# Splitting the output projection's weights during the V projection, and taking the last four heads' inverse sums on their output tiles

## The chip, the cores and the metric

The kernel runs on one core of one Trainium2 chip. The metric is the device time of one execution in microseconds. The kernel before takes 1146.8 us (median of three runs, 1144.13 to 1148.85).

## The reference, cut to what matters

One transformer block on x of shape [1, 2048, 640]: sliding-window attention with 32 heads of 20 columns and a window of 256, then a gated MLP that mixes tokens.

```python
def _A_ref(x, wqkv, wo):
    B, S, D = x.shape
    H = 32; Dh = D // H; W = 256
    qkv = (lambda x, *d: x.transpose(*d))((x @ wqkv).reshape(B, S, 3, H, Dh), 2, 0, 3, 1, 4)
    q, k, v = qkv[0], qkv[1], qkv[2]
    scores = jnp.einsum("bhqd,bhkd->bhqk", q, k) * (Dh ** -0.5)
    idx = jnp.arange(S)
    mask = (idx[:, None] - idx[None, :] >= 0) & (idx[:, None] - idx[None, :] < W)
    scores = jnp.where(mask[None, None], scores, -1e9)
    p = _softmax(scores, axis=-1)
    o = jnp.einsum("bhqk,bhkd->bhqd", p, v)
    return (lambda x, *d: x.transpose(*d))(o, 0, 2, 1, 3).reshape(B, S, D) @ wo
...
x = A_x
h = x + _A_ref(_layernorm(x, axis=-1), A_wqkv, A_wo)
h2 = h + _B_ref(_layernorm(h, axis=-1), B_w_in, B_w_sp, B_b_sp, B_w_out)
```

`_B_ref` projects to 1728 columns with a GELU, normalises one half, mixes it over tokens with a 2048x2048 matrix, multiplies with the other half and projects back. The change is in the first half, up to `o @ wo`.

## The kernel before, in words

All tensors are fp32. A product with full precision is made of two fp32r parts, a high one (a rounded copy) and a low one (the rest), as high x high, high x low and low x high. Making the parts of a tile is called a split: one copy and one subtraction.

The stages follow each other. The V projection goes over 16 tiles of 128 tokens: each tile of x is loaded, normalised on DVE, transposed on PE, split by ACT and DVE into the tiles `xa` and `xb`, and multiplied with the split `wv`. Then come the q and k products, whose three-part results go through DRAM (`qk_d`).

Attention takes eight groups g of four heads, and for each 16 tiles of keys, which makes 128 units u. A step s of its loop does four max items for unit s + 17 (a PE product and a row maximum on DVE, L312), four score items for unit s (a PE product and the exponential on ACT, L369; after the fourth, POOL masks the tile, L371 and L374), and the product with V for unit s - 2. A column of ones beside V makes the softmax sum come out as row 20 of a head's 32 output rows. After every fourth unit the function `put` copies 512 tokens of four heads from PSUM into two output tiles `ot{g}_{c}_{j}` (c the 512 tokens, j the half) and stores them in DRAM (`o_d`). Three slots in SBUF hold the operands of a group. Slot 0 and slot 2 lie at the left, slot 2 in the old `xb`; they are free after groups 6 and 5. In the last 17 steps no max items are left, so DVE has only the copies of output tiles.

There also stand, before the change, the preparations for the output projection, in the generators `inverse_sums` and `proj_early`, which advance once per step. `inverse_sums(c)` starts when group 7 has written its output tiles for c: it loads the sums of all 32 heads from `o_d` (`inv`, 128x128), takes the reciprocal on DVE (L348) and stores it in `r_d`. `proj_early` starts at step 112: it loads the five row tiles of `wo` and splits them on DVE (L182, L183) into the tile `t1`, loads the outputs of the first 512 tokens (`load_o`) and then normalises and splits tiles 0 and 1 on DVE (`norm_o` L148, `split_o` L154 and L157). The raw `wo` rows lie for that time in `m1`, where `load_o` loads too, and in `wraw`, where `w_in` is loaded afterwards.

The output projection goes over 16 tiles i: PE multiplies the split outputs with the split `wo` (`wo_ps`, L91), DVE adds x (`xh`, L1160) and takes the statistics for the next layer norm (L75, L76), POOL makes the scale, DVE applies it (L81), PE transposes (`ht_ps`, L806) and ACT copies. A PSUM tile of `wo_ps` is free for the product two tiles later when `xh` has read it. Between these stand on DVE, ACT and POOL the split of tile i + 2 and so on, and of `w_in` and the first inputs of the next stage (`zl`, `aw`, L675).

The order of the instructions is the written one on PE, DVE and ACT up to attention's end, and on SP (the queue that issues nearly all DMAs) from attention's start to step 112. Everywhere else a scheduler orders them, and it may put later work between earlier rows. Each engine then runs its own list strictly in order.

## Time and profile before

| | us |
|---|---|
| median of the runs | 1146.8 |
| the profiled execution | 1140.25 |
| its span, first to last instruction | 1138.5 |
| PE busy | 1094.5 |
| DVE busy | 746.0 |
| ACT busy | 534.6 |
| POOL busy | 405.2 |
| attention's last product with V before the output projection starts | 460.10 |
| first and last start of `wo_ps` | 463.8 and 556.4 |

Times within the execution count from its first instruction. Rows of a timeline give the start, the duration, the engine, the line, the operation, what it writes and reads by the program's names (with the numbers at their ends left out, so `t` is `t1` and `m` is `m1`), and in brackets how long the engine was idle before and what ended that. Rows of waits give the total, how often, and the longest.

### The profile page before, as it was taken

Reading aid. Unit: us, or ns where it says so; the run is one execution under the profiler, and the core shown is the slowest. Engines: PE = TensorE matmul, PEld = TensorE weight load, DVE = VectorE, ACT = ScalarE, POOL = GpSimd, SP = SyncE. Lnnn points to the kernel's source line nnn. Section 1 sums busy time; section 2 is a strip of 40 time slices with the busy share of each in tenths; the row PEclk is TensorE's granted clock in tenths of the full one; section 3 lists DMA queues with packets and bytes.
Section 4 is the critical chain, followed back from the end, with each engine's and each line's share of the span. In section 5 each row is a group of like instructions: output and inputs, shape, how many; then the busy total and the mean of one; then the engine's idle time right before and its main releaser. Section 6 shows DMA issues by size and latency. Waiting matters only on the chain. (4 is left out here: it accounts for less than half of the span.)

```text
span 1138.5 us, 27633 instructions
## 1 busy us (share of the span) xinstructions
PE 1094.5 (96%) x10652; PEld 982.7 (86%) x10652; DVE 746.0 (66%) x1963; ACT 534.6 (47%) x1165; POOL 405.2 (36%) x553
## 2 busy tenths in 40 slices
PE   6999999999999999888999998999999899999998
PEld 6998887668888886788999997999999799999998
DVE  5541223889999996599677489455558974556542
ACT  3333433259999999344366454333334421222210
POOL 4114444457777778366230363000126410000000
PEclk9999999999999999899999998999999999999999
DMA  6212565655666635588455411324331572444322
GB/s 197 70 36 86 168 225 165 212 201 187 215 211 204 199 131 193 177 291 269 163 187 182 165 51 37 103 102 136 112 112 53 170 235 91 127 142 145 99 74 78
DMA packets 83845, 170.84 MB, mean 150 GB/s; under 512 B 11009, under 2 KB 47361, under 8 KB 79873
## 3 DMA queue, kind: packets, MB, share of 16 engines
q1 hardware_dynamic: 81408, 163.83, 44.5%
q10 hardware_dynamic: 2304, 5.24, 1.2%
q8 instruction: 83, 1.36, 0.5%
q14 instruction: 50, 0.40, 0.1%
HBM read 112.37 MB, written 56.23 MB: 148 GB/s over the span
## 5 line engine op out<-in xcount | busy, mean ns | idle before, releaser
L369 ACT ACTIVATE pt<-bank 128x384 f32<-128x384 f32 (+2 forms) x512 | 200.7, 498 | 9.3 <-PE bank L366 5.1
L1013 PE MATMUL g<-zl,aw 128*128 128x432 f32 x768 | 174.4, 363 | 7.3 <-ACT zl L681 4.9
L681 ACT ACTIVATE aw<-fx 128x512 fp32r<-128x512 f32 (+2 forms) x160 | 92.7, 595 | 186.6 <-PE g L1013 121.4
L312 DVE CUSTOM_DVE_ANT_0 junk<-bank,strip 128x288 bf16<-128x288 f32 x392 | 157.6, 454 | 3.7 <-PE bank L300 1.4
L1013 PEld LDWEIGHTS g<-zl,aw 128*128 128x128 f32 x768 | 144.9, 190 | 16.1 <-ACT zl L681 5.9
L1013 PE MATMUL g<-ze,aw 128*128 128x432 f32 x576 | 138.2, 368 | 5.1 <-DVE row L675 2.9
L675 DVE TENSOR_TENSOR aw<-fx,aw 128x512 fp32r<-128x512 f32 (+2 forms) x152 | 108.4, 721 | 35.7 <-ACT aw L681 35.4
L394 PE MATMUL pv<-pt,v_sb 128*32 128x192 f32 (+3 forms) x1984 | 127.2, 322 | 2.6 <-POOL pt L371 1.9
L1013 PEld LDWEIGHTS g<-ze,aw 128*128 128x128 f32 x576 | 109.3, 192 | 12.9 <-ACT y_sp L124 1.9
L366 PE MATMUL bank<-slot 123*32 123x288 bf16 (+5 forms) x1536 | 106.6, 280 | 1.9 <-issue 0.7
L371 POOL TENSOR_SCALAR_AFFINE_SELECT pt<-pt 128x512 f32<-128x512 f32 x128 | 84.0, 656 | 45.0 <-ACT pt L369 44.0
L1052 PE MATMUL out_ps<-wout,y_sp 128*128 128x320 f32 (+1 forms) x630 | 96.2, 310 | 0.4 <-ACT y_sp L124 0.4
L1052 PEld LDWEIGHTS out_ps<-wout,y_sp 128*128 128x128 f32 (+1 forms) x630 | 94.1, 188 | 1.3 <-ACT y_sp L124 0.7
L917 PE MATMUL zb<-win,aw 128*128 128x432 f32 x480 | 95.2, 359 | 0.0
L917 PEld LDWEIGHTS zb<-win,aw 128*128 128x128 f32 x480 | 90.1, 188 | 4.4
L300 PE MATMUL bank<-slot 120*32 120x288 bf16 (+2 forms) x1264 | 88.2, 283 | 1.6 <-DVE mcol L312 1.0
L498 DVE TENSOR_TENSOR rest<-qk,sg 128x512 f32<-128x512 f32 x40 | 27.7, 692 | 86.1 <-ACT sg L496 86.0
L374 POOL TENSOR_SCALAR_AFFINE_SELECT pt<-pt 128x512 f32<-128x512 f32 x112 | 72.3, 645 | 0.0
L675 DVE TENSOR_TENSOR row<-g,row 128x432 f32<-128x432 f32 x80 | 48.0, 603 | 36.4 <-PE g L1013 32.0
L501 POOL TENSOR_TENSOR sg<-rest,sg 128x512 bf16<-128x512 f32 x40 | 46.6, 1165 | 69.7 <-ACT sg L500 63.1
L366 PEld LDWEIGHTS <-slot 123*32 123x32 bf16 x1536 | 53.2, 96 | 17.3 <-issue 6.2
L394 PEld LDWEIGHTS pv<-pt,v_sb 128*32 128x32 f32 x1984 | 59.9, 110 | 8.4 <-POOL pt L371 3.8
(189 smaller groups left out, 2172.2 us busy)
## 6 DMA issues: line engine op xcount, KB each, us to landing
fx<-wsp_in SPq DMA_DIRECT2D x32, 512.0 KB
slot<-qk_d SPq DMA_DIRECT2D x72, 200.0 KB
qk_d<-sg SPq DMA_DIRECT2D x32, 384.0 KB
slot<-qk_d SPq DMA_DIRECT2D x72, 160.0 KB
fx<-hn_d SPq DMA_DIRECT2D x32, 320.0 KB
o_d<-ot SPq DMA_DIRECT2D x64, 128.0 KB
z_d<-row SPq DMA_DIRECT2D x16, 432.0 KB
g_d<-row SPq DMA_DIRECT2D x16, 432.0 KB
```

The costliest lines, as they stand in the source:

```text
L300: nc.tensor.matmul(ps[32 * j:32 * j + 32, :n], part(st, half, 120, 0, hh, q0, 32), part(st, half, 120, 1, hh, lo + skip * j, n), start=Tru ...
L312: nc.vector.tensor_tensor_reduce(out=junk[:, :n], in0=ps[:, :n], in1=keep, scale=1.0, scalar=NEG, op0=OP.add, op1=OP.max, accum_out=m_cols ...
L366: nc.tensor.matmul(ps[32 * i:32 * i + 32, b:e], part(st, half, 123, 1, hh, k0, 32), part(st, half, 123, 0, hh, kb * P + b, e - b), start=T ...
L369: nc.scalar.activation(pt[:, hh, :n], ps[:, :n], AF.Exp, scale=SCALE)
L371: nc.gpsimd.affine_select(out=pt[:, :, :P], in_=pt[:, :, :P], pattern=[[0, 4], [1, P]], base=0, channel_multiplier=-1, compare_op=OP.is_ge ...
L374: nc.gpsimd.affine_select(out=pt[:, :, 256:], in_=pt[:, :, 256:], pattern=[[0, 4], [-1, P]], base=-1, channel_multiplier=1, compare_op=OP. ...
L394: nc.tensor.matmul(ps[32 * hh:32 * hh + 32, a - 512 * c:b - 512 * c], v_sb[:, kb, v0:v0 + 32], pt[:, hh, a - kb * P:b - kb * P], start=fir ...
L675: (eng or nc.vector).tensor_tensor(out=out, in0=a, in1=b, op=op)
L681: nc.scalar.activation(out, a, AF.Copy)
L917: nc.tensor.matmul(b[0][:, :HF], a[t][:, x, kk], win2[0][:, y, kk, h * HF:(h + 1) * HF], start=kk + x + y == 0, stop=kk == KD - 1 and x == 1)
L1013: nc.tensor.matmul(ps, w[m][:, x, k], zc[k][m][:, y], start=start and k + x + y == 0, stop=stop and k == 3 and x == 1, skip_group_check=True)
L1052: nc.tensor.matmul(ps[j][:, :HD], src[:w, a, k, :], e1["wout"][:w, b, k, j * HD:(j + 1) * HD], start=(k == 0 and a + b == 0), stop=(k == K ...
```

## The change

Four things are done.

- `wo` is loaded and split during the V projection, in iterations 1 to 7: `load_wo` brings the five row tiles, `split_wo` makes the high part on ACT and the low part on POOL, in buffers that the `wq` tiles use later, and stores both in DRAM (`wo_d`). In attention's steps from 97 on, `load_wo_parts` loads the ten parts, one a step, into `xb`, which has been free since group 5. The loads and splits in `proj_early` go.
- The tile `t1` goes. `wo`'s parts and the split outputs (`osp_parts`) lie in `xb`, which is kept to the end of the projection. `wraw` lies in the pool that `xh2` to `xh4` come from.
- `inverse_sums` serves only the first 28 heads. It starts when group 6, not group 7, has written c, waits five steps before its load and three before the reciprocal.
- For group 7, `put` takes the reciprocal of the whole output tile (`rt`, 128x256, L410 in the new file) and stores its four rows of sums in `r_d`.

```diff
@@ attention's output tiles and inverse sums
         def inverse_sums(c):
-            t = tmp3.tile([P, P], F32, tag="inv", bufs=2, name=f"inv{c}")
+            t = tmp3.tile([P, P], F32, tag="inv", bufs=2, name=f"inv{c}")[:4 * (H - 4)]
 
             def rows(d, step):
-                return bass.AP(tensor=d.tensor, offset=d.offset, ap=[[step, H], [P, 4], [1, P]])
-
+                return bass.AP(tensor=d.tensor, offset=d.offset, ap=[[step, H - 4], [P, 4], [1, P]])
+
+            for _ in range(5):
+                yield
             nc.sync.dma_start(t, rows(o_d[:, DH, c * 512:(c + 1) * 512], 32 * S))
+            for _ in range(3):
+                yield
+            nc.vector.reciprocal(out=t, in_=t)
             yield
-            yield
-            nc.vector.reciprocal(out=t, in_=t)
             nc.sync.dma_start(rows(r_d[:, c * 512:(c + 1) * 512], S), t)
             yield
...
                     nc.sync.dma_start(o_d[4 * g:4 * g + 4, :, e:e + 256].rearrange("h d t -> (h d) t"), ot)
+                    if g == 7:
+                        rt = tmp3.tile([P, 256], F32, tag="rt", bufs=2, name=f"rt{c}_{j}")
+                        nc.vector.reciprocal(out=rt, in_=ot)
+                        nc.sync.dma_start(r_d[4 * g:4 * g + 4, e:e + 256], rt[DH:P:32])
...
-                if g == 7:
+                if g == 6:
                     inverse.append(inverse_sums(c))
@@ wo in the V projection
+            def load_wo(k):
+                raws["o", k] = tmp.tile([P, D], F32, tag="wraw", bufs=4, name=f"woraw{k}")
+                nc.sync.dma_start(raws["o", k], wo[k * P:(k + 1) * P, :])
+
+            def split_wo(k):
+                raw = raws.pop(("o", k))
+                hi, lo = (tmp.tile([P, D], F32R, tag=tag, bufs=4, name=f"{tag}o{k}") for tag in ("wqh", "wql"))
+                nc.scalar.activation(hi, raw, AF.Copy)
+                nc.gpsimd.tensor_tensor(out=lo, in0=raw, in1=hi.bitcast(F32), op=OP.subtract)
+                nc.sync.dma_start(wo_d[0, k], hi.bitcast(F32))
+                nc.sync.dma_start(wo_d[1, k], lo.bitcast(F32))
...
+                if 1 <= i <= KD:
+                    load_wo(i - 1)
...
+                if 3 <= i < KD + 3:
+                    split_wo(i - 3)
@@ the parts in xb
-        mem["t1"] = pl.tile([P, 2 * KF * D], F32R, name="t1")
...
-        mem["wraw"] = pl.tile([P, 2, 2, HF], F32, name="wraw")
...
-    def t1(lo, *shape):
-        return view(mem["t1"], lo, *shape)
+    def wo_part(p, k):
+        return mem["xb"][p][:, k * D:(k + 1) * D]
+
+    def osp_parts(i):
+        if i % 3 == 2:
+            return [x[:, 7 * D:8 * D].rearrange("p (k t) -> p k t", k=KD) for x in mem["xb"]]
+        o = view(mem["xb"][i % 3], KD * D, 2, KD, P)
+        return [o[:, 0], o[:, 1]]
...
+    def load_wo_parts():
+        for k in range(KD):
+            for p in range(2):
+                nc.sync.dma_start(wo_part(p, k).bitcast(F32), wo_d[p, k])
+                yield
...
-        xb = pool(lowx, "xb")
-        xb = [xb.tile([P, CH], F32R, name=f"xb{i}") for i in range(2)]
+        xb = pool(early_stack, "xb")
+        xb = mem["xb"] = [xb.tile([P, CH], F32R, name=f"xb{i}") for i in range(2)]
...
+            if s > 6 * NT:
+                next(wo_loads, None)
...
-    mem["osp2"] = ep.tile([P, 2, KD, P], F32R, name="osp2")
+    mem["wraw"] = ep.tile([P, 2, 2, HF], F32, name="wraw")
@@ proj_early
-        for k in range(KD):
-            raw = raws_c.pop(f"wo{k}")
-            nc.vector.tensor_copy(wo_s[:, 0, k], raw)
-            nc.vector.tensor_tensor(out=wo_s[:, 1, k], in0=raw, in1=wo_s[:, 0, k].bitcast(F32), op=OP.subtract)
-            if k in (1, 3):
-                yield
-        yield
         rs = load_o(0)
-        yield
         yield
         rs()
         yield
-        yield
         load_o(1)()
-        yield
+        for _ in range(6):
+            yield
         for i in range(2):
             norm_o(i, nc.vector)
             split_o(i, nc.vector)
```

Three places show how the rows move. The first is DVE in attention's last steps, from the first output tiles of group 7 on. Before:

```order
L410 COPY ot7_0_1_9100<-pv7_0_8981 128x256
L182 CAST t1_8919<-m1_8920 128x640
L183 TENSOR_TENSOR t1_8919<-m1_8920,t1_8919 128x640
...
L182 CAST t1_8919<-wraw_8926 128x640
L183 TENSOR_TENSOR t1_8919<-wraw_8926,t1_8919 128x640
L348 RECIPROCAL inv0_9107<-inv0_9107 128x128
L410 COPY ot7_1_0_9247<-pv7_1_9061 128x256
L410 COPY ot7_1_1_9250<-pv7_1_9061 128x256
L348 RECIPROCAL inv1_9253<-inv1_9253 128x128
```

Now:

```order
L406 COPY ot7_0_0_9151<-pv7_0_9033 128x256
L410 RECIPROCAL rt0_0_9154<-ot7_0_0_9151 128x256
L406 COPY ot7_0_1_9157<-pv7_0_9033 128x256
L410 RECIPROCAL rt0_1_9160<-ot7_0_1_9157 128x256
L344 RECIPROCAL inv2_8844<-inv2_8844 112x128
L406 COPY ot7_1_0_9297<-pv7_1_9115 128x256
L410 RECIPROCAL rt1_0_9300<-ot7_1_0_9297 128x256
L406 COPY ot7_1_1_9303<-pv7_1_9115 128x256
L410 RECIPROCAL rt1_1_9306<-ot7_1_1_9303 128x256
L344 RECIPROCAL inv3_9021<-inv3_9021 112x128
```

The ten splits of `wo` are gone from here, a reciprocal stands behind each copy of an output tile, and `inv0` and `inv1` have moved ahead (`inv0` among the last row maxima). All reciprocals of the first 28 heads are done before the output tiles for c = 2.

The second place is DVE at the start of the projection; the rows with `m1` are `norm_o`, the row that waits for the most DMAs is the one for tile 2. Before:

```order
L348 RECIPROCAL inv1_9253<-inv1_9253 128x128 [waits DMAHW2_49]
L148 TENSOR_TENSOR m1_8920<-m1_8920 128x5x128 [waits DMAHW4_49,DMAHW3_49,DMAHW7_49,DMAHW1_49,DMAHW0_49]
L154 CAST t1_8919<-m1_8920 128x640 [waits DVE_49]
L157 TENSOR_TENSOR t1_8919<-m1_8920,t1_8919 128x640 [waits DVE_49]
L148 TENSOR_TENSOR m1_8920<-m1_8920 128x5x128
L148 TENSOR_TENSOR m1_8920<-m1_8920 128x5x128 [waits DMAHW4_49,DMAHW5_49,DMAHW3_49,DMAHW7_49,DMAHW1_49,DMAHW0_49]
```

Now:

```order
L410 RECIPROCAL rt2_0_9445<-ot7_2_0_9442 128x256 [waits DMAHW4_49,Activation_49]
L410 RECIPROCAL rt2_1_9451<-ot7_2_1_9448 128x256 [waits DMAHW0_49,DVE_49,Activation_49]
L153 TENSOR_TENSOR m1_8976<-m1_8976 128x5x128 [waits DMAHW5_49,DMAHW2_49,DMAHW1_49]
L153 TENSOR_TENSOR m1_8976<-m1_8976 128x5x128 [waits DMAHW4_49,DMAHW6_49,DMAHW3_49,DMAHW7_49,DMAHW2_49,DMAHW1_49]
L153 TENSOR_TENSOR m1_8976<-m1_8976 128x5x128
L159 CAST xb0_95<-m1_8976 128x640 [waits DVE_49]
```

In place of `inv1`, which waits for a DMA, two reciprocals stand ahead, which wait for ACT; and the normalisations of tiles 2 and 3 have moved ahead of tile 0's cast (tile 1 now comes after it).

The third place is DVE at the first two additions of x. Before:

```order
L348 RECIPROCAL inv2_9398<-inv2_9398 128x128
L1160 TENSOR_TENSOR xh0_8921<-wo_ps0_9473,xh0_8921 128x640
L75 BN_STATS stc0_9608<-xh0_8921 128x6 x2
L76 BN_AGGR mvc0_9609<-stc0_9608 128x2
L81 TENSOR_SCALAR m1_8920<-xh0_8921,mvc0_9609 128x640
L1160 TENSOR_TENSOR xh1_8922<-wo_ps1_9518,xh1_8922 128x640
L75 BN_STATS stc1_9624<-xh1_8922 128x6 x2
L148 TENSOR_TENSOR m1_8920<-m1_8920 128x5x128 x2
L348 RECIPROCAL inv3_9549<-inv3_9549 128x128
```

Now:

```order
L1173 TENSOR_TENSOR xh0_8977<-wo_ps0_9525,xh0_8977 128x640
L76 BN_STATS stc0_9665<-xh0_8977 128x6
L410 RECIPROCAL rt3_0_9570<-ot7_3_0_9567 128x256
...
L153 TENSOR_TENSOR m1_8976<-m1_8976 128x5x128 x2
L410 RECIPROCAL rt3_1_9576<-ot7_3_1_9573 128x256
L77 BN_AGGR mvc0_9666<-stc0_9665 128x2
L1173 TENSOR_TENSOR xh1_8978<-wo_ps1_9579,xh1_8978 128x640
...
L76 BN_STATS stc1_9681<-xh1_8978 128x6 x2
L82 TENSOR_SCALAR m1_8976<-xh0_8977,mvc0_9666 128x640
```

`inv2` and `inv3` are gone, `rt3_0` and `rt3_1` and the normalisations of tiles 4 and 5 now stand ahead of `xh1`, and the use of tile 0's statistics has moved behind `xh1`.

More of the change, by code (lines that the diff above doesn't have):

```diff
@@ L56, in block_kernel @@
     g_d = dram.tile([NT, P, FH], F32, name="g_d")
+    wo_d = dram.tile([2, KD, P, D], F32, name="wo_d")
     ident = const.tile([P, P], F32, name="ident")
@@ L151, in split_o @@
         ot, _ = ots[i]
-        osp = mem["osp2"] if i % 3 == 2 else t1((2 * KD + i % 3 * 2) * D, 2, KD, P)
+        osp = osp_parts(i)
         if eng is nc.vector:
-            eng.tensor_copy(out=osp[:, 0], in_=ot)
+            eng.tensor_copy(out=osp[0], in_=ot)
         else:
-            nc.scalar.activation(osp[:, 0], ot, AF.Copy)
-        eng.tensor_tensor(out=osp[:, 1], in0=ot, in1=osp[:, 0].bitcast(F32), op=OP.subtract)
+            nc.scalar.activation(osp[0], ot, AF.Copy)
+        eng.tensor_tensor(out=osp[1], in0=ot, in1=osp[0].bitcast(F32), op=OP.subtract)
         ots[i] = osp
@@ L161, in proj_o @@
         osp = ots.pop(i)
[L162 to L175 removed]
+        gemm(ps, HD, [lambda k, p=p: osp[p][:, k, :] for p in range(2)],
+             [lambda k, j, p=p: wo_part(p, k)[:, j * HD:(j + 1) * HD] for p in range(2)], KD)
+        return ps
+    def load_wo_parts():
[3 more added lines that the diff above has]
+                yield
+    def proj_early():
         for i in range(2):
             load_x2(i)
[L178 removed]
+        for _ in range(6):
             yield
[L180 to L186 removed]
         rs = load_o(0)
[L188 removed]
         yield
@@ L191, in proj_early @@
         yield
-        yield
         load_o(1)()
-        yield
+        for _ in range(6):
+            yield
         for i in range(2):
@@ L201, in block_kernel @@
     with ExitStack() as ab:
-        lowx, low0, high, x01, b1 = (ab.enter_context(ExitStack()) for _ in range(5))
+        low0, high, x01, b1 = (ab.enter_context(ExitStack()) for _ in range(4))
         tmp2 = pool(high, "tmp2", side="right")
@@ L651, in block_kernel @@
             pass
-        for f in inverse:
-            for _ in f:
-                pass
     ms.close()
```

17 lines of the change are left out of this document (2 added, 15 removed).

## The prediction

> **What bounds the kernel now.** I read the stretches first. The table of windows lists per row the stretch (us), its length, the busy time of PE, PEld, DVE, ACT and POOL with instruction counts, the granted clock, the DMA share and GB/s.
>
> ```profile
> core 0: us, PE busy (x) PEld busy (x) DVE busy (x) ACT busy (x) POOL busy (x), PEclk, DMA share, GB/s
> 20.00:80.00 60.00, 60.00 (x426) 59.93 (x425) 31.35 (x76) 20.25 (x49) 10.26 (x26) 1.00 0.20 56
> 245.00:434.00 189.00, 186.11 (x5282) 153.58 (x5278) 184.44 (x930) 180.21 (x477) 141.93 (x271) 1.00 0.57 183
> 434.00:461.00 27.00, 23.41 (x517) 13.83 (x509) 12.86 (x18) 24.66 (x67) 23.50 (x35) 1.00 0.65 217
> 461.00:472.00 11.00, 8.21 (x50) 7.82 (x51) 8.31 (x10) 1.88 (x4) 2.02 (x2) 0.69 0.54 161
> 472.00:542.00 70.00, 61.60 (x410) 59.37 (x409) 65.69 (x106) 26.54 (x48) 43.08 (x41) 0.98 0.81 266
> 542.00:557.00 15.00, 15.00 (x109) 14.98 (x108) 10.50 (x21) 2.86 (x4) 5.27 (x11) 1.00 0.58 215
> 557.00:1138.50 581.50, 565.04 (x3053) 537.94 (x3051) 360.20 (x603) 210.51 (x400) 96.59 (x84) 0.99 0.37 120
> ```
>
> The V projection (20 to 80) is PE alone. In attention (245 to 434) DVE, with its row maxima, is busy 98%, and PE and ACT nearly as much. In its tail (434 to 461), where no maxima are left, ACT and POOL set the pace. Then comes a hole (461 to 472), and from 472 to 542, the output projection, DVE is at 94% and PE at 88%. The change touches the first five rows; the 581 us behind keep their instructions.
>
> Next, PE's longest wait from 461 to 558 (total, times, longest), and the ends of the projection stage on DVE and on PE:
>
> ```profile
> PE wo_ps L91 <- DVE xh L1160: 6.7, 5, 3.0
> ```
> ```profile
> 540.77 0.81 DVE L1160 TENSOR_TENSOR xh<-wo_ps,xh 128x640 f32<-128x640 f32 x1
> ```
> ```profile
> 541.63 2.46 PE L91 MATMUL wo_ps<-t 128*128 128x320 f32 x15 [1.30 <-DVE xh L1160]
> ```
>
> PE is held by the residual additions `xh`. The one at 540.77 belongs to tile 11; after it PE runs on without a break. So the stage ends when DVE has finished `xh11`, and a microsecond there is a microsecond at the end.
>
> **The change, part by part.** (a) Splitting wo during the V projection adds five ACT copies and five POOL subtractions of 128x640, with ten stores and five loads on SP. The same shapes stand in the trace:
>
> ```profile
> L474 ACT ACTIVATE wqh<-wqraw x10: 729/731/742, 79.3 to 178.0; 128x640 fp32r<-128x640 f32 x10
> L475 POOL TENSOR_TENSOR wql<-wqraw,wqh x10: 1560/1569/1584, 80.1 to 179.8; 128x640 fp32r<-128x640 f32 x10
> ```
>
> That is 5 x 0.73 = 3.7 us on ACT and 5 x 1.57 = 7.8 us on POOL, against 20.3 and 10.3 busy of 60 while PE is full. In ACT's queue each copy stands behind the evacuations that the next product needs. On SP the stores come ahead of later x loads, but those wait for the normalisation three tiles on anyway. Cost 0; with the cover gone it would be 7.8 us. The ten later loads of the parts go out at attention's group 6, spread among o_d stores, where slots are no longer loaded: 0.
>
> (b) The four reciprocals of the first 28 heads come earlier; `inv0` now stands between the last row maxima, where DVE is full:
>
> ```profile
> 420.00:430.00 10.00, 10.00 (x288) 8.21 (x281) 9.84 (x50) 9.71 (x25) 8.16 (x17) 1.00 0.15 46
> ```
> ```profile
> L348 DVE RECIPROCAL inv<-inv x4: 952/953/953, 453.5 to 481.6; 128x128 f32<-128x128 f32 x4
> ```
>
> At most 0.95 us, at least 0 if the banks ahead of it absorb it; I take +0.7.
>
> (c) The ten wo instructions leave DVE at 442.7 to 452.4, and this is where I see the gain. POOL's mask over the same time, DVE's split, and the reciprocal behind it:
>
> ```profile
> 440.73 0.63 POOL L371 TENSOR_SCALAR_AFFINE_SELECT pt<-pt 128x512 f32<-128x512 f32 x1 [0.37 <-ACT pt L369]
> ...
> 442.26 0.63 POOL L371 TENSOR_SCALAR_AFFINE_SELECT pt<-pt 128x512 f32<-128x512 f32 x1 [0.31 <-ACT pt L369]
> ...
> 447.70 1.21 POOL L371 TENSOR_SCALAR_AFFINE_SELECT pt<-pt 128x512 f32<-128x512 f32 x1
> ...
> 453.47 0.63 POOL L371 TENSOR_SCALAR_AFFINE_SELECT pt<-pt 128x512 f32<-128x512 f32 x1
> ...
> 456.21 0.64 POOL L371 TENSOR_SCALAR_AFFINE_SELECT pt<-pt 128x512 f32<-128x512 f32 x1 [0.31 <-ACT pt L369]
> ```
> ```profile
> 447.29 1.13 DVE L183 TENSOR_TENSOR t<-m,t 128x640 fp32r<-128x640 f32 x1
> ...
> 453.50 0.95 DVE L348 RECIPROCAL inv<-inv 128x128 f32<-128x128 f32 x1 [1.07 <-DMA inv<-o_d]
> ```
> ```profile
> ACT pt L369 <- PE bank L366: 0.9, 4, 0.3
> ```
>
> A mask takes 1.21 us instead of 0.63 while DVE casts and subtracts, and 0.63 beside the reciprocal. With the masks late PE is late, and ACT, which sets the tail, idles 0.9 us in four waits. The masks of two tiles start 1.53 us apart at 440.73 and 442.26; the eight tiles from 442.26 to 456.21 took 13.95 instead of 12.24, so the loss is 0.9 to 1.7; I take -1.1. Where the masks waited, only copies from PSUM and reciprocals stand now. [...]
>
> (d) The handover. ACT, DVE and PE there:
>
> ```profile
> 457.40 0.78 ACT L408 ACTIVATE ot<-pv 128x256 f32<-128x256 f32 x2
> ```
> ```profile
> 461.25 0.95 DVE L348 RECIPROCAL inv<-inv 128x128 f32<-128x128 f32 x1 [6.20 <-DMA inv<-o_d]
> 462.12 0.76 DVE L148 TENSOR_TENSOR m<-m 128x640 f32<-128x640 f32 x1
> 462.92 0.82 DVE L154 CAST t<-m 128x640 fp32r<-128x640 f32 x1
> ```
> ```profile
> 460.10 0.53 PE L394 MATMUL pv<-pt,v_sb 128*32 128x192 f32 x8 [0.22 <-POOL pt L371]
> 463.79 7.19 PE L91 MATMUL wo_ps<-t 128*128 128x320 f32 x30 [3.16 <-DVE t L154]
> ```
>
> Before, tile 0's normalisation was stuck on DVE behind `inv1`, which waited 6.20 us for its load. That wait goes, but the order shows what is late next: two reciprocals of 128x256, `rt2_0` and `rt2_1`, now stand there, and they need the output tiles that ACT writes at 457.40; behind them come the normalisations of tiles 0, 2 and 3 before tile 0's cast. No row has a 128x256 reciprocal. Its price lies between 0.95 (no growth with the width) and 1.91 (twice); I take 1.85, almost twice, since 0.95 for 128 columns, against 0.76 for a multiplication of 640 columns at 462.12, says that it is paid by the column. With (b) and (c) the first tile is there at 457.8 - 0.4 = 457.4; 2 x 1.85 + 3 x 0.76 brings the cast to 463.4, and PE starts 0.87 later as before: 464.3 against 463.79, +0.5 (both ends of the reciprocal: -1.3 to +0.6). The normalisation of tile 2 needs loads that stand on SP behind `rt1_1`'s store. The product that ends this tile's sums:
>
> ```profile
> 449.81 0.64 PE L394 MATMUL pv<-pt,v_sb 128*32 128x256 f32 x8 [0.16 <-POOL pt L374]
> ```
>
> From 450.5 two copies of 0.35 and two reciprocals take DVE to 454.9, and the loads have 7 us to land.
>
> The first product takes 7.19 us because of the clock:
>
> ```profile
> 463.00:469.00 6.00, 5.21 (x19) 5.21 (x20) 4.49 (x6) 0.74 (x1) 0.50 (x1) 0.50 0.60 174
> ```
> ```profile
> 471.39 4.67 PE L91 MATMUL wo_ps<-t 128*128 128x320 f32 x30
> ```
>
> Half speed costs it 2.5 us against the second. The hole stays, so I leave that loss: product 0 ends at 464.3 + 7.2 = 471.5. [...]
>
> (e) The projection stage. Before, `inv2` kept DVE, and `xh0` started late, after product 0 had ended at 471.0:
>
> ```profile
> 472.46 0.76 DVE L1160 TENSOR_TENSOR xh<-wo_ps,xh 128x640 f32<-128x640 f32 x1
> ```
>
> Now it starts at 471.5: -0.95. From `xh0` to `xh11` the instructions are the same on both orders, less `inv3` (0.95) and plus `rt3_0` and `rt3_1` (2 x 1.85): +2.75. Against it stands DVE's idle time in that stretch:
>
> ```profile
> DVE m L148 <- DMA m<-o_d: 1.9, 1, 1.9
> DVE m L81 <- POOL mvc L78: 1.7, 2, 1.0
> DVE inv L348 <- DMA inv<-o_d: 1.1, 2, 0.8
> DVE m L148 <- issue: 0.2, 1, 0.2
> ```
>
> 4.9 us, of which 0.8 is `inv2`'s ahead of `xh0`: 4.1. The added reciprocals and an earlier w_in split fill it: `xh1` and two normalisations now stand between a tile's statistics and its use, and the loads of tiles 4 and 5 no longer share SP with `inv2`. I take 3.5 of it back (0 to 4.1): -0.75, bounds +2.75 to -1.35.
>
> Sum: to `xh0` -0.95, which holds (b), (c) and (d); the stage -0.75; -1.7 together. The profiled execution, 1140.25 (span 1138.5), becomes 1138.5. It lies 6.5 below the median shown, 1146.8, which becomes **1145**.
>
> **Rivals.** One, *DVE meets POOL less in the projection stage*, faster. DVE's operations are stretched there too:
>
> ```profile
> L148 DVE TENSOR_TENSOR m<-m 128x640 f32<-128x640 f32 x12 | 10.5, 907 | 2.1 <-DMA m<-o_d 1.9 <-issue 0.2
> L81 DVE TENSOR_SCALAR m<-xh,mvc 128x640 f32<-128x640 f32 x10 | 10.0, 1005 | 1.7 <-POOL mvc L78 1.7
> ```
> ```profile
> L81 DVE TENSOR_SCALAR m<-xh,mvc x10: 553/606/1856, 475.4 to 534.5; 128x640 f32<-128x640 f32 x10
> ```
>
> Against 0.76 (the row at 462.12) and 0.61 (the median) these two groups lose 12 x 0.15 + 10 x 0.4 = 5.8 us. The new order of all rows after attention is another draw. If it saved all of that, -7.5 in total: 1139. Against it: the same POOL work must fit the same stage.
>
> Two, *DVE waits at its head for loads of o*, slower. The normalisations of tiles 4 to 7 now stand one place earlier on DVE, and on SP the loads for 6 and 7 stand behind `rt3_0`'s store, which waits for DVE. If each of the two pairs comes 3 us late, DVE, the bound, loses 6, and `rt3` costs its full 2.75 with nothing recovered: -0.95 + 2.75 + 6 = +7.8, 1154.6. It decides once those loads take over 3.6 us from issue to landing; the row above shows one such wait of 1.9.
>
> Three, *the tail doesn't speed up*, because the reciprocals stretch the masks as the casts did: 1.1 is not gained, the sum is -0.6: 1146.2. The mask of 0.63 at 453.47 beside a reciprocal speaks against it.
>
> **The numbers.** Forecast 0.62, less meeting 0.14, late loads 0.10, no tail gain 0.14. The range takes the bounds (about -5 to +4) and part of the first two rivals, with some spread of the runs, which lie 4.7 apart: 1139 to 1151. What this kernel's measurement can tell from no change is 0.5%, 5.7 us: faster means below 1141.1, slower above 1152.5. Most of rival one is faster, 0.12 in all; most of rival two slower, 0.08; the rest 0.80.
>
> **What would show it.** Masks of 0.63 throughout the tail and no ACT idle there (c); `rt` rows of 1.85 us with the cast right behind `rt2_1` and three normalisations, and PE's start near 464 (d); `xh0` without a wait on DVE and DVE without idle until `xh11`, which ends near 540 (e); PE full to 80 us (a). I am wrong if a reciprocal of 256 columns is far from 1.85, if PE starts before 462, or if DVE waits for o_d loads in the projection.

## The result and the profile after

The changed kernel takes 1150.37 us (median of 14 runs, 1147.76 to 1154.12), the kernel before 1143.95 in its 14 runs: a ratio of 1.0062 with a 95% interval of 1.0046 to 1.0078. It is slower by 0.6%, some 6.4 us. The forecast was 1145, a gain of 1.7; the direction was wrong.

The profiled executions lie 13.9 apart, 1154.12 (span 1152.4) against 1140.25. To see where, cut both at the same five instructions: the start of the last row maximum on DVE, which ends attention's full part, the last product of attention with V, the first product of the output projection, and the first and the last residual addition (`xh0`, `xh15`). The rows of the two DVE ends, the first two of the kernel before, the others of the changed one:

```profile
432.79 0.45 DVE L312 CUSTOM_DVE_ANT_0 junk<-bank,strip 128x288 bf16<-128x288 f32 x1
...
556.77 0.82 DVE L1160 TENSOR_TENSOR xh<-wo_ps,xh 128x640 f32<-128x640 f32 x1 [0.84 <-PE wo_ps L91]
```
```profile
438.45 0.45 DVE L306 CUSTOM_DVE_ANT_0 junk<-bank,strip 128x288 bf16<-128x288 f32 x1
...
480.96 0.82 DVE L1173 TENSOR_TENSOR xh<-wo_ps,xh 128x640 f32<-128x640 f32 x1 [2.90 <-PE wo_ps L92]
...
568.80 0.82 DVE L1173 TENSOR_TENSOR xh<-wo_ps,xh 128x640 f32<-128x640 f32 x1 [0.78 <-PE wo_ps L92]
```

Up to the last row maximum the changed kernel is 5.7 us later, from there to `xh15` 6.4 longer (130.35 against 123.98), and behind `xh15` 1.9 longer. The first and the third piece are mostly the spread of single executions: in the fourteen profiles of this study the last row maximum starts at 432.8 to 436.5 in the four kernels without the new sums and at 434.0 to 441.0 in the ten with them, and what follows `xh15` takes 579.9 to 585.5. The middle piece is the change's, and it alone is as large as the difference of the medians (as near as single executions tell).

The hole in the changed kernel as a window (stretch, length, busy time of PE, PEld, DVE, ACT and POOL with counts, granted clock, DMA share, GB/s), and PE's two ends of it:

```profile
464.60:474.00 9.40, 0.03 (x4) 0.00 (x0) 6.47 (x6) 0.74 (x1) 0.73 (x2) 0.68 0.43 132
```
```profile
464.10 0.53 PE L390 MATMUL pv<-pt,v_sb 128*32 128x192 f32 x8 [0.22 <-POOL pt L367]
474.05 0.90 PE L92 MATMUL wo_ps<-xb 128*128 128x320 f32 x2 [9.42 <-DVE xb L159]
```

PE stands still for 9.4 us between attention and the projection, where it stood 3.16 before. DVE in that hole, first row to last:

```profile
464.72 1.75 DVE L410 RECIPROCAL rt<-ot 128x256 f32<-128x256 f32 x1 [2.34 <-DMA r_d<-rt]
...
471.71 1.56 DVE L153 TENSOR_TENSOR m<-m 128x640 f32<-128x640 f32 x2 [2.11 <-DMA o_d<-ot]
473.19 0.81 DVE L159 CAST xb<-m 128x640 fp32r<-128x640 f32 x1
```

DVE waits three times, twice for the store of an earlier `rt` tile (there are two buffers) and then at the pair of normalisations of tiles 2 and 3, whose data aren't there. The last row names a store of an output tile as what ended that wait; the profile infers this, and in e2_norm_early, e7_rt_copy and e9_rt_own_two the same wait ends with the load of the inverse sums (`m<-r_d`), which is issued here at 468.05. Tile 0's cast, for which PE waits, stands behind that pair.

Piece by piece, from the anchors named: last row maximum to last product with V 25.65 (before 27.3), -1.65; from there to the projection's first product 9.95 (3.69), +6.26; to `xh0` 6.91 (8.67), -1.76; `xh0` to `xh15` 87.84 (84.31), +3.53. Together +6.4.

### The profile page after: what moved, and what is told of

Same layout as the page of the kernel before. It is cut to its first block, busy times and chain, and to the rows that moved or that the text cites. A ratio compares the mean times of both kernels' runs of the same rounds, so it can differ in the third digit from the quotient of the medians.

```text
span 1152.4 us, 27709 instructions
## 1 busy us (share of the span) xinstructions
PE 1096.0 (95%) x10652; PEld 983.6 (85%) x10652; DVE 750.0 (65%) x1961; ACT 538.3 (47%) x1170; POOL 409.3 (36%) x558
## 3 DMA queue, kind: packets, MB, share of 16 engines
q8 instruction: 84, 1.38, 0.5%
## 5 line engine op out<-in xcount | busy, mean ns | idle before, releaser
L362 PE MATMUL bank<-slot 123*32 123x288 bf16 (+6 forms) x1536 | 109.0, 282 | 3.9 <-issue 1.7
L367 POOL TENSOR_SCALAR_AFFINE_SELECT pt<-pt 128x512 f32<-128x512 f32 x128 | 81.5, 637 | 50.4 <-ACT pt L365 49.6
L370 POOL TENSOR_SCALAR_AFFINE_SELECT pt<-pt 128x512 f32<-128x512 f32 x112 | 71.4, 638 | 0.0
```

What stands on the lines that cost most here:

```text
L362: nc.tensor.matmul(ps[32 * i:32 * i + 32, b:e], part(st, half, 123, 1, hh, k0, 32), part(st, half, 123, 0, hh, kb * P + b, e - b), start=T ...
L367: nc.gpsimd.affine_select(out=pt[:, :, :P], in_=pt[:, :, :P], pattern=[[0, 4], [1, P]], base=0, channel_multiplier=-1, compare_op=OP.is_ge ...
L370: nc.gpsimd.affine_select(out=pt[:, :, 256:], in_=pt[:, :, 256:], pattern=[[0, 4], [-1, P]], base=-1, channel_multiplier=1, compare_op=OP. ...
```

## The experiments

Two theories stood after this. *Buffers*: two `rt` buffers are too few, and DVE waits at them. *Order and loads*: tile 0's cast stands behind tiles 2 and 3, whose loads come late for another reason. The table gives the places of each profiled execution, from the start of its last row maximum, and the ratio of the medians; each place comes from one execution.

| kernel | last pv | first wo product | xh0 | xh15 | ratio |
|---|---|---|---|---|---|
| before | 27.3 | 31.0 | 39.7 | 124.0 | 1 |
| changed | 25.65 | 35.6 | 42.5 | 130.35 | 1.0062 |
| e1_rt8 | 25.5 | 31.1 | 39.05 | 124.7 | 1.0057 |
| e2_norm_early | 25.9 | 28.1 | 38.8 | 124.9 | 1.001 |
| e3_wo_only | 32.5 | 33.3 | 39.5 | 123.6 | 1.0011 |
| e4_sums_only | 35.3 | 37.8 | 44.2 | 132.4 | 1.0117 |
| e5_rt_own | 25.5 | 31.5 | 38.2 | 124.7 | 1.0008 |
| e6_norm_rt_own | 25.9 | 26.3 | 34.6 | 118.8 | 0.9973 |
| e7_rt_copy | 25.85 | 32.6 | 39.9 | 125.4 | 1.001 |
| e8_wo_norm_early | 25.6 | 28.45 | 37.1 | 129.9 | 1.005 |
| e9_rt_own_two | 25.5 | 31.4 | 38.15 | 124.2 | 0.9994 |
| e10_norm_rt_load | 25.7 | 26.05 | 35.8 | 118.9 | 0.9958 |
| e11_rt_ho | 25.5 | 35.6 | 42.5 | 130.2 | 1.0058 |
| e12_wo_late | 32.4 | 33.2 | 39.0 | 126.2 | 1.003 |

### e1_rt8: eight buffers for rt

```diff
-  rt = tmp3.tile([P, 256], F32, tag="rt", bufs=2, ...)
+  rt = tmp3.tile([P, 256], F32, tag="rt", bufs=8, ...)
```

> The changed kernel with eight buffers for the inverted output tiles rt instead of two; nothing else. Theory A, the two buffers: in the profile of the change DVE waited 6.7 us in four places for the store of the rt two before. With a buffer for each, those waits go, rt2_0 starts right behind ACT's output copy, PE starts wo_ps0 about 5 us earlier (469 instead of 474) and the time falls from 1150.4 to about 1145.4. Theory B, the order on SP and DVE: between 454.5 and 468.6 SP issues 19 transfers at 0.6 to 0.75 us each, and the loads that tiles 2 and 3 need stand last among them; these two tiles' normalisations stand ahead of tile 0's cast, so DVE then waits there instead, PE starts at 471 to 473, and the time is 1148 to 1149.5. Theory C, attention itself has become slower (its last product ended 4.0 us later in the profile): the handover changes nothing that counts beyond that, and 1150 stays.

Measured: 1148.89 against 1142.54, ratio 1.0057 (1.0039 to 1.0075). The waits at `rt` are gone and the hole is short again, but the time isn't better. The larger pool moved attention's tiles in memory: the first exponentials now wait for a store of a staging tile of q and k (4.09 us), and PE behind them.

```profile
250.70 2.47 ACT L365 ACTIVATE pt<-bank 128x384 f32<-128x384 f32 x6 [4.09 <-DMA qk_d<-sg]
```

So the run doesn't tell the theories apart: what it gained at the handover it lost at attention's start. The time lies in theory B's range, but not for theory B's reason, since DVE waits only 1.38 us at tiles 2 and 3. Nor is the short hole the buffers' doing alone: the larger pool also moved five loads on SP behind the handover (issued at 487.7 to 489.7), the same five that e9_rt_own_two is about.

### e2_norm_early: tiles 0 and 1 normalised ahead

```diff
         rs()
         yield
-        load_o(1)()
-        for _ in range(6):
+        for _ in range(3):
             yield
         for i in range(2):
             norm_o(i, nc.vector)
             split_o(i, nc.vector)
             yield
+        load_o(1)()
```

> The changed kernel with tile 0's and tile 1's normalisation and split asked for earlier (three steps behind the load of the sums, not seven) and the loads for tiles 2 and 3 behind them. On DVE tile 0's normalisation, cast and subtraction now stand ahead of rt2_0 and rt2_1. The rt buffers stay two. Theory B: tile 0 needs only what has long landed, PE starts wo_ps0 at about 464.5, right behind attention's last product; DVE reaches xh0 when rt2, two normalisations and tile 1's split are done, at about 474 to 475 instead of 481; time 1143 to 1145. Theory A: DVE's waits for the rt stores stay and hold rt1 and rt2 as before; PE's early start gains nothing, since xh0 stands behind rt2 on DVE: xh0 at 478 or later, 1147 to 1150. Theory C: 1150, with attention's end where it was.

Measured: 1144.28, ratio 1.001 (0.9993 to 1.0028), no longer slower than before. The waits at `rt` stay (3.29 us at one of them); what changed is that tile 0's cast no longer stands behind tiles 2 and 3. PE's first product:

```profile
465.80 0.61 PE L92 MATMUL wo_ps<-xb 128*128 128x320 f32 x2 [1.68 <-DVE xb L159]
```

The order theory can explain the loss without the buffers.

### e3_wo_only and e4_sums_only: one part alone

The changed kernel with the old `inverse_sums` for all 32 heads and no `rt`:

```diff
-  t = tmp3.tile([P, P], F32, tag="inv", ...)[:4 * (H - 4)]
+  t = tmp3.tile([P, P], F32, tag="inv", ...)
...
-  if g == 7:
-      rt = ...; nc.vector.reciprocal(out=rt, in_=ot); nc.sync.dma_start(r_d[...], rt[DH:P:32])
...
-  if g == 6:
+  if g == 7:
       inverse.append(inverse_sums(c))
```

> The changed kernel with the inverse sums as they were before the change (all 32 heads in one load behind group 7, no rt): the split of wo in the V projection and its loads in parts alone. If the handover is the cost of the change (A and B), this kernel has it not: 1142 to 1144, the tail's 1 us gained or lost in the spread, and a hole of 3 us or less at the handover. If the loads of the wo parts or the stack memory that wo keeps slow attention down (C), attention ends 3 to 4 us later than before here too, and the time is 1147 to 1149.

And the kernel before with the new sums, the same lines the other way round:

```diff
+  t = tmp3.tile([P, P], F32, tag="inv", ...)[:4 * (H - 4)]
...
+  if g == 7:
+      rt = ...; nc.vector.reciprocal(out=rt, in_=ot); nc.sync.dma_start(r_d[...], rt[DH:P:32])
...
-  if g == 7:
+  if g == 6:
       inverse.append(inverse_sums(c))
```

> The kernel before with the new inverse sums alone (28 heads behind group 6, the last four on their output tiles); wo is loaded and split in the tail as before. A and B: rt stands on DVE with its two buffers and the ten wo instructions between them: a hole of 9 us or more at the handover, time 1150 to 1154. C: the hole is there but attention ends where it did before, 1146 to 1148.

Measured: the split alone 1142.78, ratio 1.0011 (0.9996 to 1.0027); the sums alone 1155.42, ratio 1.0117 (1.0096 to 1.0138). The first says that splitting `wo` during the V projection costs nothing, as forecast, and gains nothing by itself: DVE, freed from the splits, only waits for the inverse sums, and ACT's cast of a tile of the projection, in its queue ahead of the last exponentials, holds them, and PE with them (4.79 us at one product of scores).

```profile
462.50 1.56 DVE L153 TENSOR_TENSOR m<-m 128x640 f32<-128x640 f32 x2 [10.19 <-DMA m<-r_d]
```
```profile
463.36 0.74 ACT L161 ACTIVATE xb<-m 128x640 fp32r<-128x640 f32 x1 [4.34 <-DVE m L153]
```

The second missed its expectation of a hole of 9 us: the hole is 1.7, and the loss lies ahead of it, where the last product with V comes 8.0 us later than before. So the new sums need the splits out of the way: with both on DVE, the copy that frees a product's bank is late.

```profile
462.72 0.66 PE L396 MATMUL pv<-pt,v_sb 128*32 128x128 f32 x8 [4.29 <-DVE ot L412]
```

The parts aren't additive (1.0011 and 1.0117 against 1.0062 together).

### e5_rt_own and e6_norm_rt_own: own buffers, without and with the early normalisation

Six `rt` tiles of their own in the pool of the early stage, and two in the old place:

```diff
+  mem["rt"] = [pl.tile([P, 256], F32, name=f"rt{i}") for i in range(6)]
+  mem["rt"] += [tmp3.tile([P, 256], F32, tag=f"rt", bufs=2, ...) for i in (6, 7)]
...
-  rt = tmp3.tile([P, 256], F32, tag="rt", bufs=2, ...)
+  rt = mem["rt"].pop()
```

> The changed kernel with eight buffers for rt as in the first experiment, but six of them in the memory that attention's slot 0 leaves, so that the tiles of attention lie where they lay. In the first experiment the tiles pt lay over the staging tiles of the q and k projection and ACT waited 4.1 us at attention's start. Theory A (DVE's waits for the rt buffers cost time): those 4.1 us and the half clock behind them go, from the last row maximum to xh15 it stays at about 124.7 us against 130.4 of the change, and the time is 1144 to 1146. If the 5.7 us of that stretch were a chance of one execution, or came from the other order of the x loads: 1148.5 to 1150.

The same with the edit of e2_norm_early (the diff shown there):

> Both repairs: tiles 0 and 1 normalised earlier (ahead of rt2), and eight buffers for rt outside the memory of attention. If the two costs are apart: PE starts wo_ps0 within 2 us of attention's last product, DVE's rt rows wait for no store, xh0 comes some 36.5 us behind the last row maximum (38.8 with the early normalisation alone), and the time is 1140 to 1142, a little under the kernel before. If the loads for tiles 2 and 3, late on SP, set DVE's time whatever the buffers do, it is no better than the early normalisation alone: 1143 to 1145.

Measured: 1142.94 against 1141.84, ratio 1.0008 (0.9996 to 1.002), and 1138.54, ratio 0.9973 (0.9955 to 0.9991), which beats both kernels; both are somewhat faster than expected. I took the first for the proof of the buffers theory. It wasn't, as the next runs show.

### e7_rt_copy: a copy in the reciprocal's place

The last four heads' sums stay uninverted here; only the instruction's length changes.

```diff
-  nc.vector.reciprocal(out=rt, in_=ot)
+  nc.vector.tensor_copy(out=rt, in_=ot)
```

> The changed kernel with a copy in place of the inversion of the last four heads' output tiles (their sums are left uninverted, so the results of these heads differ): the same tiles, buffers and transfers, but about 0.35 instead of 1.75 us for each rt on DVE. If DVE's own time for the inversions is the cost, 2.8 us go ahead of tile 0's cast and 2.8 in the projection stage: 1144 to 1146. If the waits for the two buffers and for the loads are, DVE waits longer in their place: PE starts wo_ps0 still 8 to 9 us behind attention's last product, 1148 to 1150.

Measured: 1143.27, ratio 1.001 (0.9997 to 1.0023). Neither theory's numbers came out: `rt` takes 0.29 to 0.57 us ahead of the projection instead of 1.75, yet PE's hole is still 6.2, and DVE waits longer than before, at `rt` and at tiles 2 and 3.

```profile
459.59 0.45 DVE L410 COPY rt<-ot 128x256 f32<-128x256 f32 x1 [5.70 <-DMA r_d<-rt]
...
466.31 1.56 DVE L153 TENSOR_TENSOR m<-m 128x640 f32<-128x640 f32 x2 [4.91 <-DMA m<-r_d]
```

The scheduler also set the stores of `rt` ahead of the loads of o here, so the run isn't a clean measure of the reciprocal. What it shows is that the stores and loads on SP are late even when DVE's work is short.

### e8_wo_norm_early: the early normalisation without the new sums

e3_wo_only with the edit of e2_norm_early, in `proj_early`:

```diff
-        load_o(1)()
-        for _ in range(6):
+        for _ in range(3):
             yield
...
+        load_o(1)()
```

> The split of wo in the V projection alone (inverse sums as before the change), with tiles 0 and 1 normalised earlier. In the profile of the split alone, ACT's cast for tile 2 stood between the last exponentials and waited 4.3 us for DVE's normalisation, which waited 10.2 us for the loads of the inverse sums; attention ended some 4.8 us late by it. If the order of the normalisations is the cost, tile 0's cast now stands right behind its normalisation and PE goes from attention to wo_ps0 without the stop: 1138 to 1141. ACT's cast for tile 2 still stands among the exponentials, though: if that sets it, 1142 to 1144.

Measured: 1147.73, ratio 1.005 (1.0036 to 1.0065), against an expected 1138 to 1144. `xh0` came 2.4 us sooner than in e3_wo_only, but the stage behind it took 92.8 instead of 84.1. Two of DVE's pairs of normalisations took 3.47 and 3.80 there (the one at 543.55 took 1.55), with POOL busy 10.53 us from 500 to 520, and PE, which waited 6.5 us for DVE's scaled tiles in two waits, had a granted clock of 0.83 in that stretch:

```profile
499.36 3.47 DVE L153 TENSOR_TENSOR m<-m 128x640 f32<-128x640 f32 x2 [2.54 <-DMA m<-o_d]
...
527.50 3.80 DVE L153 TENSOR_TENSOR m<-m 128x640 f32<-128x640 f32 x2
```
```profile
500.00:520.00 20.00, 15.73 (x97) 15.71 (x98) 19.12 (x33) 8.92 (x17) 10.53 (x10) 0.83 0.79 257
```

The early normalisation is no gain in itself; it pays with the new sums. That POOL's work stretched the pairs is an estimate from these lengths and POOL's busy time; why they are longer in this order wasn't tried.

### e9_rt_own_two: the memory of e5_rt_own, but two tiles in use

```diff
-  rt = mem["rt"].pop()
+  rt = mem["rt"][6 + j]
```

> The memory of the fifth experiment (eight tiles for rt, six of them outside attention's), but only two of them in use by turns, so that the rt of a tile waits again for the store of the rt two before. On SP the loads of x for tiles 2 to 4 and of w_in stand behind the handover, as in the fifth experiment; in the change they stand ahead of it. If the wait for the two buffers was what the fifth experiment took away (6.2 us of time): 1148 to 1149.5, DVE's rt rows wait for r_d stores in three or four places. If it was the loads of x and w_in (1.4 MB ahead of the o_d stores in the change), which delay the landings: 1143 to 1144.5, though DVE still waits here and there.

Measured: 1142.85 against 1142.38, ratio 0.9994 (0.9977 to 1.001). Two buffers are enough. So what else had e5_rt_own changed? The orders of DVE, ACT and POOL equal the changed kernel's up to `xh0`. On SP five loads differ: `x` for three tiles (320 KB each) and two of `w_in` (432 KB each), 1.82 MB together (not the 1.4 of the expectation). With the six added tiles in the pool they go out behind the handover, at 481 to 483; in the changed kernel they are issued at 441 to 448, ahead of the store of group 7's first output tile (`ot7_0_0`). SP of the changed kernel, then of this one (start, time of issue):

```profile
445.43 1.26 SPq L346 DMA_DIRECT2D r_d<-inv  x1
446.74 0.53 SPq L134 DMA_DIRECT2D xh<-x_in  x1
447.31 0.90 SPq L755 DMA_DIRECT2D wraw<-w_in_in  x2
449.16 0.85 SPq L341 DMA_DIRECT2D inv<-o_d  x1
450.11 0.50 SPq L407 DMA_DIRECT2D o_d<-ot  x1
454.46 0.59 SPq L141 DMA_DIRECT2D m<-o_d  x1
455.10 0.58 SPq L411 DMA_DIRECT2D r_d<-rt  x1
...
465.33 0.55 SPq L411 DMA_DIRECT2D r_d<-rt  x1
...
468.05 0.59 SPq L147 DMA_DIRECT2D m<-r_d  x1
```
```profile
442.01 0.86 SPq L348 DMA_DIRECT2D r_d<-inv  x1
444.31 0.83 SPq L343 DMA_DIRECT2D inv<-o_d  x1
445.23 0.50 SPq L409 DMA_DIRECT2D o_d<-ot  x1
448.40 0.59 SPq L143 DMA_DIRECT2D m<-o_d  x1
449.09 0.58 SPq L413 DMA_DIRECT2D r_d<-rt  x1
...
460.70 0.60 SPq L149 DMA_DIRECT2D m<-r_d  x1
...
481.07 1.45 SPq L136 DMA_DIRECT2D xh<-x_in  x3
482.61 1.31 SPq L757 DMA_DIRECT2D wraw<-w_in_in  x2
```

The copy that fills this first output tile starts at 447.55 in the changed kernel and at 444.32 here. Its store is issued 2.56 us behind it there and 0.91 here: ahead of it SP stands at the load of the next inverse sums, whose buffer the store at 445.43 must leave first (3.73 us from that store's issue to the load's, 2.30 here). Then SP reaches a load that needs the output tile's store, and waits at its head: 4.35 us from the store's issue to the load's (450.11 to 454.46), 3.17 here. Together the load comes 2.83 us later. All that SP has behind it moves with it: the stores of `rt`, which DVE then waits for at two buffers, and the loads of o and of the inverse sums. By the last one that tiles 2 and 3 need (468.05 and 460.70) the delay against the copy is 4.1, and tile 0's cast is as late, 34.7 us behind the last row maximum against 30.5. What the DMA engines carry from 440 to 446, in the changed kernel and here:

```profile
440.00:446.00 6.00, 5.90 (x133) 3.83 (x126) 1.90 (x4) 6.00 (x17) 4.69 (x9) 1.00 0.81 270
```
```profile
440.00:446.00 6.00, 5.82 (x128) 3.79 (x125) 1.81 (x3) 6.00 (x18) 4.79 (x8) 1.00 0.33 105
```

Both stores land later with the loads in flight, by 1.4 and 1.2 us as SP's two waits give it. Whether that comes from the bytes that the loads move, or from something else that their place changes, wasn't tried apart.

### e11_rt_ho: own buffers, and nothing else moved

Each `rt` beyond the first two lies in a tile that isn't in use yet, so that no pool grows:

```diff
+  if c == 0:
       rt = tmp3.tile([P, 256], F32, tag="rt", bufs=2, ...)
+  else:
+      rt = mem["ho"][c - 1][:, 256 * j:256 * j + 256]
```

> The changed kernel with a buffer of its own for each rt (two as before, six in the halves of the three tiles ho that lie idle until the third product), and nothing else moved: up to xh0 all engines and SP have the change's order, the loads of x for tiles 2 to 4 and of w_in too. The ninth experiment moved those five loads and left the two buffers; this one does the opposite. If the loads alone made the loss, DVE's waits for rt go but those for the loads of o stay as late: 1148 to 1150. If either the wait for the buffers or the loads has to go, and one is enough: 1143 to 1145, as with the loads moved.

Measured: 1148.78 against 1142.03, ratio 1.0058 (1.0036 to 1.008), the changed kernel's. No `rt` waits any more, but the wait has only gone on to tiles 2 and 3, and PE starts as late (35.6 behind the last row maximum, as in the changed kernel):

```profile
470.46 1.56 DVE L153 TENSOR_TENSOR m<-m 128x640 f32<-128x640 f32 x2 [5.88 <-DMA o_d<-ot]
```
The buffers theory falls: e9_rt_own_two keeps two buffers and is rid of the loss, this kernel has eight and keeps it. With e5_rt_own, whose SP has the five loads behind the handover too, all four cases are there: the loads early, 1.0062 with two buffers and 1.0058 with eight; the loads late, 0.9994 and 1.0008.

### e12_wo_late: late loads for the old sums

Is it simply good to have the five loads late? e3_wo_only with 8 KB a partition left empty in the pool, so that they move behind the handover:

```diff
+  pl.tile([P, 8 * 256], F32, name="pad")
```

> The split of wo alone (third experiment, 1142.8) with two kilobytes a partition of memory left unused among the early tiles, times four, so that the loads of x for tiles 2 to 4 and of w_in fall behind the handover as in the ninth experiment. If these loads delay the small transfers at the handover whatever the sums do, DVE's wait of 10.2 us for the loads of the inverse sums and ACT's of 4.3 get shorter here too: 1138 to 1141. If the old path (sums to memory, loaded, inverted, stored, loaded) is long enough by itself, nothing: 1142 to 1144.

Measured: 1145.48, ratio 1.003 (1.0014 to 1.0046): no gain, rather a small loss, and slower than both expectations. With the old sums the chain through the last inverse is what DVE waits for (10.37 us at `m<-r_d`, 10.19 in e3_wo_only), whatever the loads do. The early loads hurt only the kernel whose sums hang on short stores behind them.

### e10_norm_rt_load: both repairs

The memory of e5_rt_own, the early normalisation, and the second load of o right behind the first:

```diff
         rs()
-        yield
         load_o(1)()
-        for _ in range(6):
+        yield
+        for _ in range(3):
             yield
```

> The sixth experiment (early normalisation, eight buffers) with the loads for tiles 2 and 3 right behind those for tiles 0 and 1 instead of behind the normalisations. In the profile of the sixth, DVE still stood 2.1 us ahead of tile 2's normalisation, 4.8 us behind attention's last product, for a load issued late. If the loads are the last wait at the handover, xh0 comes 2 us earlier and the time falls to 1136 to 1138. If on SP the output tiles' stores, which now stand behind these loads, come late instead, DVE and PE wait for them: 1139 to 1142.

Measured: 1136.88 against 1142.38, ratio 0.9958 (0.994 to 0.9976), the fastest of all. PE goes from attention into the projection without a wait:

```profile
459.91 1.12 PE L392 MATMUL pv<-pt,v_sb 128*32 128x192 f32 x16
460.96 0.56 PE L92 MATMUL wo_ps<-xb 128*128 128x320 f32 x2
```

Of the 5.1 us that it is ahead of the kernel before at `xh15`, 3.9 are there at `xh0`. The interval overlaps that of e6_norm_rt_own (0.9955 to 0.9991); which place of the second load is better stays open.

## Why the prediction was wrong

**(a) The split of wo, 0: right.** PE stays full from 20 to 80, ACT's and POOL's added work (3.2 and 7.9 us) lies beside it, and e3_wo_only, which keeps this part, takes the kernel before's time.

```profile
20.00:80.00 60.00, 60.00 (x426) 59.94 (x426) 31.34 (x75) 23.47 (x54) 18.15 (x31) 1.00 0.42 139
```

**(b) `inv0` between the row maxima, +0.7: not measurable.** It is 0.95 us of DVE, and the last row maximum's place varies by 3.7 us between the four executions that don't have it.

**(c) The tail, -1.1 with 1.7 as its end: right, at the upper end.** It took 1.65 less. POOL's masks from the last row maximum on, in the changed kernel (group: busy, mean ns, idle before):

```profile
L367 POOL TENSOR_SCALAR_AFFINE_SELECT pt<-pt 128x512 f32<-128x512 f32 x17 | 10.8, 637 | 5.2 <-ACT pt L365 5.2
```

A mean of 0.64 leaves no stretched mask. Beside the reciprocals of `rt`, too, the masks keep 0.64 (the one at 448.38, beside the reciprocal from 448.00 to 449.75). Why they took up to 1.21 beside casts and subtractions before and don't beside a reciprocal, no run shows. Rival three, in which the tail gained nothing, falls with this.

**(d) The handover: here it failed.** The reciprocal was sized well (1.75 for 1.85), and so was every other length on DVE. DVE's four waits for the two `rt` buffers, 6.7 us in all, were not in the sum, but e11_rt_ho, which is without them, is as slow. The step that failed is "the loads have 7 us to land". I took DVE's time at which `rt1_1` would be ready (454.9 on the time axis of before) as the time at which SP would store it. But SP was not at that store: it had issued big loads ahead, and stood at its head at a load that needs an output tile's store to land. The working named SP's queue for what stands behind `rt1_1`'s store, not for what stands ahead of it, and gave the store no time to land. In the changed kernel that store is issued at 465.33 and the last load that tiles 2 and 3 need at 468.05 (the SP rows of e9_rt_own_two's section); counted from the last row maximum, that is 459.7 and 462.4 on the time axis of before, 4.8 and 7.5 us behind the 454.9 from which I let the loads run. Of the 10 us from the last product with V to PE's start 4.6 were forecast. e9_rt_own_two, with only the five loads moved, starts 5.9 behind it, and 31.4 behind the last row maximum, where the kernel before starts 31.0. So with the loads moved 4.2 of the 6.3 lost in this hole are gone, and what is left goes with the order: e6_norm_rt_own, with both repairs, has no hole. The two aren't shares that add up, since the order alone (e2_norm_early, with the loads still early) also takes the whole loss here away. The rows of before had shown this wait: two stores at 444.09, then SP stands until 449.11, with loads of `x` and `w_in` ahead there too.

```profile
439.59 2.68 SPq L129 DMA_DIRECT2D xh<-x_in  x3
443.24 0.33 SPq L742 DMA_DIRECT2D wraw<-w_in_in  x1
444.09 0.80 SPq L411 DMA_DIRECT2D o_d<-ot  x2
449.11 0.60 SPq L136 DMA_DIRECT2D m<-o_d  x1
```

There the chain through `inv1` was later still, so the wait set nothing, and I did not carry it over.

The clock in and behind the hole, from two windows of the changed kernel:

```profile
468.10:474.05 5.95, 0.00 (x0) 0.00 (x0) 3.81 (x6) 0.74 (x1) 0.66 (x1) 0.50 0.40 123
474.05:478.25 4.20, 4.02 (x14) 3.62 (x15) 3.94 (x4) 0.00 (x0) 0.88 (x1) 0.50 0.15 43
```

Of 10.2 us at half clock 6.0 fell into the hole itself, where they cost nothing, and `xh0` starts 6.91 behind the first product, where I had put 7.2. The slow stretch as a whole is longer than before (10.2 us against 6.8 there, from 462.6 to 469.4), but the added time lies where PE waits anyway.

**(e) The projection stage, -0.75 to `xh11`: wrong.** In the profiled execution `xh11` starts 69.73 behind `xh0`, 1.4 more than before (68.31): inside the bounds, with the wrong sign. From there to `xh15` it is another 2.1 longer (18.11 against 16.00), where I had put nothing because PE ran on without a break before. `rt3`'s two reciprocals less `inv3` are +2.55 at their measured length; the recovery of 3.5 from DVE's idle time did not come. The whole stage, before and changed:

```profile
472.46:556.77 84.31, 75.91 (x512) 73.66 (x511) 75.50 (x125) 29.13 (x51) 47.89 (x51) 0.98 0.78 258
480.96:568.80 87.84, 77.57 (x533) 74.84 (x533) 78.07 (x126) 30.32 (x54) 47.54 (x51) 0.98 0.74 244
```

DVE is busy 2.6 us longer, as long as the added reciprocals, and instead of idling less it idles 9.8 us where it idled 8.8. The loads of o no longer make it wait here, but POOL's statistics do so more, before and changed:

```profile
DVE m L81 <- POOL mvc L78: 4.2, 6, 1.0
```
```profile
DVE m L82 <- POOL mvc L79: 6.9, 9, 1.0
```

With the loads late (e9_rt_own_two) the stage took 86.05, 1.7 more than before. Why DVE waits more for POOL isn't settled: e8_wo_norm_early shows that this stage can vary by 8 us with the order alone (92.8 against 84.1 in e3_wo_only).

**The rivals.** Rival two (late loads of o at DVE's head) had the right mechanism and the right side, at another place: I set it at tiles 4 to 7 in the projection, behind `rt3_0`'s store, and it came at tiles 2 and 3, before PE's first product, where it costs most. It had a chance of 0.10, too little for a kernel in which a new chain of store, load, store, load had been laid on one queue. Rival one, less meeting with POOL, did not show: DVE's scalings by the statistics took 1.00 us on average in this stage, 0.96 before.

**Slower or not.** That the change as a whole is a loss is true of this arrangement only. Its parts are worth 0.4% (e10_norm_rt_load) once tile 0 is normalised first and the loads go out later. By itself, neither the split (e3_wo_only) nor the whole change with late loads (e9_rt_own_two) beat the kernel before.

## What to carry to other kernels

When sums or tiles go through DRAM at a handover, walk the issuing queue as carefully as an engine: list every transfer ahead of the one that is needed, with its issue time, and give each dependent load the time for the store before it to land, since the queue stood at it here (4.35 us from the store's issue to the load's in the changed kernel) and everything behind was late. A wait for a buffer can be a symptom of that; give the buffer away without moving anything else, and see whether the wait only moves on. And if a pool grows, compare the order of all queues before taking the result as the effect of the buffers.

## What the runs showed of the hardware that I had not expected

The granted clock fell at a wait of under 2 us as well. In e6_norm_rt_own PE waited 1.78 us up to 467.25; the clock was 1.00 from 464 to 467, 0.64 from 467 to 470 and 0.50 from 470 to 474:

```profile
467.25 0.53 PE L92 MATMUL wo_ps<-xb,xb 128*128 128x320 f32 x2 [1.78 <-DVE xb L161]
```
```profile
464.00:467.00 3.00, 1.47 (x23) 1.01 (x22) 2.19 (x3) 1.27 (x2) 0.51 (x1) 1.00 0.20 54
467.00:470.00 3.00, 2.15 (x8) 1.81 (x9) 2.96 (x4) 0.76 (x3) 3.00 (x2) 0.64 0.16 44
470.00:474.00 4.00, 4.00 (x16) 4.00 (x16) 3.47 (x4) 0.00 (x0) 0.14 (x1) 0.50 0.76 253
```

PE was busy 1.47 of the 3 us up to 467, just ahead of the fall. In e2_norm_early, behind a wait of 1.68 us, the clock was 0.72 from 464 to 470, and two products took 0.73 us at 466.21 against 0.46 at 470.42. Which part of the waiting makes the clock fall, no run shows.

A reciprocal on DVE took nearly twice the time for twice the columns, 0.95 us for 128 and 1.75 for 256, where the eight copies of 256 columns in e7_rt_copy took 0.27 to 0.98, half of them under 0.42.
